# Left-over tokens of a top-1 mixture of experts: first and last item in conditional blocks, the last one in plain float32 column tiles

## The chip, the cores and the metric

One core of one Trainium2 chip runs the whole kernel. The metric is device time in microseconds (us) of one execution, as the median of three runs.

## What is computed

Sigmoid attention over 8 batches of 12 heads with 448 tokens of 64 features, then a mixture of 8 experts over the 3584 tokens of 768 features, where each token goes to its best expert alone. All is float32.

```python
scores = scale * q @ k.T - log(S)
attn = 1 / (1 + exp(-scores));  x = attn @ v        # heads side by side: 3584 x 768
logits = x @ w_gate                                  # 8 experts
expert_idx = argmax(logits);  gate_w = softmax(logits)[expert_idx]
for e in range(8):
    xe = x[expert_idx == e]
    h = maximum(xe @ w1[e], 0)                       # w1[e]: 768 x 1024
    out[expert_idx == e] = gate_w * (h @ w2[e])      # w2[e]: 1024 x 768
```

## The kernel before

Attention runs pair of heads by pair of heads (scores L534, sigmoid L521, weighted values L548), in plain float32 on quadrants of 64 x 64 of TensorE's array. The experts run batch by batch: each batch's 448 tokens go through the expert that most of them chose (w1 at L218, w2 at L237), and the attention of later batches is interleaved with that. Every float32 operand of the experts is cut into a high and a low float32r part (ScalarE casts, L143, VectorE subtracts, L144), and a product is the sum of three matmuls, high x high, high x low, low x high. A unit of weights is such a pair of 512 columns, made from half of a raw tile of 512 KB that SP loads (L136, L166).

Tokens that chose another expert than their batch's are recorded, with gate, in a table in memory (recs). What is left over is done at the end, as items: up to 256 rows of one expert. While the last batch's experts run, VectorE makes the list of items (L706 to L742): items of over 128 rows come first, then the smaller ones; li holds their numbers and experts, ki how many there are of each sort. With the inputs used there are two items, worked out from the reference: 218 rows of expert 7 and 1 row of expert 3.

An item's body is `item(i, nh, ...)` (L843), nh halves of 128 rows. The rows' x is the stationary operand and w1, split into w1h and w1l for all 1024 columns beforehand, moves with 512 columns (L854). Each half of h is turned by four transposes (L900) and split again (L903), since h must be stationary for w2, whose units are split as the body goes on. VectorE or ScalarE multiply by the gate (L938 for VectorE) into xo, and GpSimd writes rows out with two indirect DMAs, the scatter (L810), that are issued at the start of the next item or behind the loops. A table, AT, says behind which matmul of an item each split of weights and of rows stands. So the first item's body also gathers, sorts and turns the rows of the second (L764 to L787), and loads and splits its w1 (L804).

Two hardware loops follow one another: items with nh = 2 (L945), then items with nh = 1 (L947). Every engine reads the loops' bounds from ki (L841) and walks through both loops; a loop's turn is a join of all engines. In the last batch, `until(n)` puts a step n matmuls ahead of that batch's last one, and `more(n)` lets n matmuls go by. There stand the gather of the first item's rows, their sorting and turning, and the loads and splits of its w1. Raw tiles come from a ring of five (wst), behind the last batch also from four tiles (hl) that the batch's h occupied.

Of the kernel before, what the change touches and what calls it, by code (L numbers as in the profile page):

```python
# [25 lines left out]
def tile_sigmoid_attention_top1_moe(  # L26
# [644 lines left out]
    for s, n in attention():  # L671
        if s >= START:
# [8 lines left out]
    ps_m2 = ctx.enter_context(tc.tile_pool(name="ps_m2", bufs=3, space=bass.MemoryType.PSUM))  # L681
    TL = 2 * P


    AT = (
        (
            dict(zip((0, 1, 2, 3, 4, 12, 5, 6, 7, 8, 13, 14, 15, 16, 9, 10, 11, 17),
                     (38, 43, 48, 54, 60, 84, 102, 108, 114, 120, 126, 132, 138, 144, 150, 156, 162, 175))),
            (74, 90, 128, 168),
        ),  # L690
        (dict(zip((0, 1, 4, 5, 8, 9, 2, 3, 6, 7, 10, 11), (16, 20, 24, 28, 33, 42, 48, 54, 60, 66, 72, 78))), ()),
    )
# [18 lines left out]
    big, few, rank = cut(4), cut(5), [cut(6), cut(7)]  # L711
    nc.vector.tensor_tensor(ek(5), ek(0), n_rec, op=ALU.is_lt)
    nc.vector.tensor_scalar(cut(0), cut(0), float(P), None, op0=ALU.add)
    nc.vector.tensor_tensor(ek(4), ek(0), n_rec, op=ALU.is_lt)
    nc.vector.tensor_sub(few, few, big)
    more(20)
    for msk, cum in zip((big, few), rank):
        nc.vector.tensor_tensor_scan(cum, cut(3), msk, 0.0, op0=ALU.mult, op1=ALU.add)
# [4 lines left out]
    for msk, cum in zip((big, few), rank):  # L723
        nc.vector.scalar_tensor_tensor(msk, cum, slot1, msk, op0=ALU.is_equal, op1=ALU.mult)
    more(20)
    nc.vector.tensor_add(big, big, few)
    prod = cut(8, 2).rearrange("p (a n) -> p a n", a=2)
    nc.vector.tensor_mul(
        prod, cut(1, 2).rearrange("p (a n) -> p a n", a=2), big.unsqueeze(1).broadcast_to([P, 2, NI])
# [4 lines left out]
    ki = rest.tile([1, 2], I32, name="ki")  # L734
    nc.vector.tensor_scalar(ends[:, 0:1], ends[:, 1:2], -1.0, ends[:, 0:1], op0=ALU.add, op1=ALU.max)
    nc.vector.tensor_copy(ki, ends[0:1])
# [9 lines left out]
    rec_s = rest.tile([P, 2, 2], U32, name="rec_s")  # L746
    rec_c = rest.tile([P, 2, 2], U32, name="rec_c")
    rec_n = rest.tile([P, 2, 2], U32, name="rec_n")
    xg = rest.tile([P, 2, DM], F32, name="xg")
# [4 lines left out]
    w1h = rest.tile([P, KD, DF], F32R, name="w1h_item")  # L754
    w1l = rest.tile([P, KD, DF], F32R, name="w1l_item")
# [7 lines left out]
    def get_rows(ireg, rec, nh):  # L763
        nc.sync.dma_start(rec, recs_v[bass.ds(ireg, 1)].rearrange("o p t w -> (o p) t w"))  # L764
        for t in range(nh):
# [9 lines left out]
    def sort_rows(nh):  # L775
        for t in range(nh):
            nc.vector.tensor_copy(
                xp[:, t].rearrange("p k (i s) -> p k i s", s=32), xg[:, t].rearrange("p (i k s) -> p k i s", i=4, s=32)
            )

    def split_rows(k2, nh):
        px = ps_x.tile([P, 512], F32, tag="px", name=f"px_{k2}")
        w = nh * P
        for kk in range(2):
            for t in range(nh):
                at = kk * w + t * P
                nc.tensor.transpose(px[:, at : at + P], xp[:, t, 2 * k2 + kk], ident)  # L787
        for kk in range(2):
            xh, xl = xrs[2 * k2 + kk]
            part = px[:, kk * w : (kk + 1) * w]  # L790
            nc.scalar.copy(xh[:, :w], part)
            nc.vector.tensor_sub(xl[:, :w], part, xh[:, :w].bitcast(F32))

    RAWS = [(wpool, "wst")] * RAWS_AHEAD
    turn = itertools.count()

    def raw_tile(name):
        pool, ring = RAWS[next(turn) % len(RAWS)]
        bufs = RAWS_AHEAD if ring == "wst" else None
        return pool.tile([P, 1024], F32, tag=ring, bufs=bufs, name=name)  # L800

    def w1_load(ereg, t):
        st = raw_tile(f"w1r_{t}")
        nc.sync.dma_start(st, w1[bass.ds(ereg, 1), t * P : (t + 1) * P, :].rearrange("e p n -> (e p) n"))  # L804
        return st

    def scatter():
        puts = []
        for t in range(2):
            put = nc.gpsimd.indirect_dma_start(  # L810
                out=out,
                out_offset=bass.IndirectOffsetOnAxis(ap=rec_s[:, t, 0:1], axis=0),
# [7 lines left out]
    nc.gpsimd.iota(rec_s, pattern=[[0, 4]], base=int(BIG), channel_multiplier=0)  # L820
    nc.gpsimd.memset(xg, 0.0)
    get_rows(item_reg(0), rec_c, 2)
    e0 = expert_reg(0)
    until(96)
    sort_rows(2)
    until(86)
    for k2 in range(KD // 2):
        split_rows(k2, 2)
        more(8)
    until(60)  # L830
    w1rs = [w1_load(e0, t) for t in range(3)]
    for t in range(KD):
        until(50 - 9 * t)
        part_split(w1rs[t], (w1h[:, t], w1l[:, t]), nc.vector)
        if t + 3 < KD:
            w1rs.append(w1_load(e0, t + 3))
    until(0)
    next(mo, None)
    order.close()
    RAWS = RAWS + [(hpool, f"hl{j}") for j in range(0, KF, 2)]  # L840
    ends_r = [nc.values_load(ki[0:1, a : a + 1], min_val=0, max_val=NI) for a in range(2)]  # L841

    def item(i, nh, split_at, sort_at):  # L843


        n = 0
        hooks = {}

        def at(m, f):
            hooks.setdefault(m, []).append(f)  # L850

        def mm(*a, **kw):
            nonlocal n
            nc.tensor.matmul(*a, **kw)  # L854
            n += 1
            for f in hooks.pop(n, ()):
                f()

        ereg = expert_reg(i)
        scatter()  # L860
        if sort_at:
            enext = expert_reg(i + 1)
            get_rows(item_reg(i + 1), rec_n, nh)
        raws, parts = {}, {}
        todo = list(dict.fromkeys(u // 2 if u < NU else NU + u for u in split_at))

        def load():
            if todo:
                r = todo.pop(0)
                if r < NU:  # L870
                    raws[r] = raw_tile(f"w2r_{r}")
                    w2_rows(ereg, r, raws[r])
                else:
                    raws[r] = w1_load(enext, r - 2 * NU)

        def split(u):
            if u < NU:
                parts[u] = part_tiles("w2", 512, f"r_{u}")
                part_split(raws[u // 2][:, u % 2 * 512 : (u % 2 + 1) * 512], parts[u], nc.vector)
            else:  # L880
                t = u - NU
                part_split(raws[NU + u], (w1h[:, t], w1l[:, t]), nc.gpsimd if t % 2 else nc.vector)
            if u >= NU or u % 2:
                load()

        for _ in RAWS:
            load()
        for u, m in split_at.items():
            at(m, lambda u=u: split(u))
        half = DF // 2  # L890
        if sort_at:
            at(sort_at[0], lambda: sort_rows(nh))
            for k2 in range(KD // 2):
                at(sort_at[1 + k2], lambda k2=k2: split_rows(k2, nh))
        hts = {}

        def turn_h(f, h, hf):
            ph = ps_x.tile([P, 512], F32, tag="px", name=f"ph_{f}_{h}")
            for c in range(4):
                nc.tensor.transpose(ph[:, c * P : (c + 1) * P], hf[:, c * P : (c + 1) * P], ident)  # L900
            two = hpool.tile([P, 1024], F32R, tag=f"hh{4 * f + 2 * h}", name=f"h_{f}_{h}")
            hh, hl = two[:, :512], two[:, 512:]
            nc.scalar.copy(hh, ph)  # L903
            nc.vector.tensor_sub(hl, ph, hh.bitcast(F32))
            hts[f, h] = hh, hl

        for f in range(2):
            for h in range(nh):
                ps = ps_moe.tile([P, 512], F32, tag="moe", name=f"ps1_{f}_{h}")
                cs = slice(f * half, (f + 1) * half)  # L910
                for t in range(KD):
                    xh, xl = (x[:, h * P : (h + 1) * P] for x in xrs[t])
                    for m, (a, b_) in enumerate(((xh, w1h), (xh, w1l), (xl, w1h))):
                        mm(ps, a, b_[:, t, cs], start=(t == 0 and m == 0), stop=(t == KD - 1 and m == 2))
                hf = opool.tile([P, 512], F32, tag="ob", name=f"hf_{f}_{h}")
                nc.scalar.activation(hf, ps, AF.Relu)
                at(n + 9, lambda f=f, h=h, hf=hf: turn_h(f, h, hf))


        order = [(d, h, jh) for d in range(ND) for h in range(nh) for jh in range(2)]  # L920
        if nh == 1:
            order.sort(key=lambda x: x[2])
        pos = {}
        for d, h, jh in order:
            if jh == 0:
                pos[d, h] = ps_m2.tile([P, 512], F32, tag="m2", name=f"ps2_{d}_{h}")
            ps = pos[d, h][:, :DW]
            for j in range(4):
                whi, wlo = (x[:, j % 2 * DW : (j % 2 + 1) * DW] for x in parts[4 * d + 2 * jh + j // 2])
# [48 lines left out]
```

## Time and profile before

| | us |
|---|---|
| median of 3 runs (smallest to largest) | 850.48 (848.18 to 853.02) |
| the profiled execution's own time | 845.28 |
| its span in the profile | 842.0 |
| last batch's last matmul ends, first item begins | 773.4 |
| first item begins to second item begins | 773.4 to 815.3 |
| second item | 815.3 to 834.0 |
| from there to the end | 834.0 to 842.0 |

The profile shows one execution on the core. PE is TensorE's matmuls, PEld its weight loads, DVE is VectorE, ACT ScalarE, POOL GpSimd, SP the engine that issues most loads. A group of instructions is named by source line, engine, operation, output <- inputs and shape; after the bar stand its busy time and the mean duration of one in ns, then the idle time in front of it and what ended that. The chain that ended last is written in order of time: start, duration, engine, what, line.

### The profile page before, as it was taken

How to read it: one execution, taken by the hardware profiler on the slowest of the kernel's cores; microseconds unless marked ns; L12 is line 12 of the kernel's file. 1: busy time of each engine (PE TensorE's matmuls, PEld its weight loads, DVE VectorE, ACT ScalarE, POOL GpSimd, SP SyncE). 2: the span in 40 equal slices, each digit the busy share in tenths (PEclk: the TensorE clock that was granted, in tenths of full speed). 3: DMA queues.
4: the chain of work that ended last, by engine and by line, in shares of the span. 5: the costliest groups of instructions: out<-in, count | busy, mean ns of one | idle time of the engine just before them, and what ended most of it. 6: DMA issues, size and time to landing. Idle time of an engine off the chain costs nothing.

```text
span 842.0 us, 15396 instructions
## 1 busy us (share of the span) xinstructions
PE 827.2 (98%) x5637; PEld 635.2 (75%) x5637; DVE 415.2 (49%) x863; ACT 398.6 (47%) x691; POOL 154.8 (18%) x221
## 2 busy tenths in 40 slices
PE   8999999999999999999999999999999999999986
PEld 6647678677678677687687687787687689998875
DVE  2456446435464355345464365353472257556544
ACT  5875634454534635445525626435526522334543
POOL 3445003110041002210041001300141005202240
PEclk9999999999999999999999999999999999999998
DMA  8999865485394574784656565675642427537523
GB/s 152 153 185 187 213 146 135 110 206 131 73 220 111 115 168 117 141 185 102 140 123 159 146 127 128 152 157 130 140 135 67 118 58 191 170 119 211 203 81 124
DMA packets 289514, 120.61 MB, mean 143 GB/s; under 512 B 204420, under 2 KB 283156, under 8 KB 289440
## 3 DMA queue, kind: packets, MB, share of 16 engines
q1 hardware_dynamic: 278176, 99.27, 50.9%
q0 software_dynamic: 9088, 19.46, 9.5%
q10 hardware_dynamic: 2176, 0.92, 0.8%
q8 instruction: 44, 0.72, 0.4%
q14 instruction: 30, 0.25, 0.1%
HBM read 97.55 MB, written 24.64 MB: 145 GB/s over the span
## 4 chain that ended last, share of the span: by engine, by line
PE 94%; DMA 3%; issue 1%; DVE 1%; ACT 1%; POOLq 0%; ACTq 0%; POOL 0%; SPq 0%; DVEq 0%
PE ps L237 28%; PE ps L218 28%; PE sc L534 15%; PE av L548 15%; PE ps L854 5%; PE psg L265 2%; DMA kn<-in_k_dram 1%; DMA first<-in_q_dram 1%; DMA out_dram<-ob 1%; DMA w2r<-in_moe_w_dram 0%; PE pl L274 0%; PE ph L900 0%; PE px L787 0%; DVE xt L411 0%; POOLq L973 0%
## 5 line engine op out<-in xcount | busy, mean ns | idle before, releaser
L521 ACT ACTIVATE at<-sc,bias_s 128x448 f32<-128x448 f32 x336 | 196.0, 631 | 133.2 <-PE sc L534 132.0
L534 PE MATMUL sc<-qt,kt 64*64 64x448 f32 x1344 | 174.8, 545 | 0.1
L548 PE MATMUL av<-at,vn 64*64 64x448 f32 x1344 | 173.1, 537 | 0.0
L253 POOL DMA_DIRECT2D out_dram<-ob x96 | 61.1, 649 | 486.2 <-DVE ob L248 407.7
L237 PE MATMUL ps<-hh,w2l 128*128 128x448 f32 x384 | 141.9, 370 | 0.0
L237 PE MATMUL ps<-hh,w2h 128*128 128x448 f32 x384 | 141.6, 369 | 0.0
L218 PE MATMUL ps<-xl,w1h 128*128 128x448 f32 x384 | 141.3, 368 | 0.0
L218 PE MATMUL ps<-xh,w1l 128*128 128x448 f32 x384 | 140.7, 366 | 0.2 <-DVE w1l L144 0.2
L237 PE MATMUL ps<-hl,w2h 128*128 128x448 f32 x384 | 140.8, 367 | 0.0
L218 PE MATMUL ps<-xh,w1h 128*128 128x448 f32 x384 | 140.4, 366 | 0.0
L557 DVE TENSOR_TENSOR xl<-av,xh 128x448 fp32r<-128x448 f32 x48 | 29.0, 605 | 216.4 <-ACT xh L556 215.0
L534 PEld LDWEIGHTS sc<-qt,kt 64*64 64x64 f32 x1344 | 79.7, 191 | 58.2 <-issue 24.0
L223 ACT ACTIVATE hh<-ps 128x448 fp32r<-128x448 f32 x64 | 34.9, 545 | 161.2 <-PE ps L218 161.1
L548 PEld LDWEIGHTS av<-at,vn 64*64 64x64 f32 x1344 | 64.3, 132 | 59.5 <-issue 26.3
L143 ACT CAST w2h<-wst 128x512 fp32r<-128x512 f32 x96 | 61.5, 658 | 86.9 <-PE ps L237 78.7
L218 PEld LDWEIGHTS ps<-xl,w1h 128*128 128x128 f32 x384 | 72.1, 188 | 10.8 <-issue 5.2
L237 PEld LDWEIGHTS ps<-hh,w2h 128*128 128x128 f32 x384 | 72.2, 188 | 9.4 <-issue 4.2
L237 PEld LDWEIGHTS ps<-hh,w2l 128*128 128x128 f32 x384 | 72.2, 188 | 8.3 <-issue 2.8
L218 PEld LDWEIGHTS ps<-xh,w1l 128*128 128x128 f32 x384 | 72.1, 188 | 8.3 <-issue 1.4
L218 PEld LDWEIGHTS ps<-xh,w1h 128*128 128x128 f32 x384 | 72.1, 188 | 6.4 <-issue 0.7
L237 PEld LDWEIGHTS ps<-hl,w2h 128*128 128x128 f32 x384 | 72.2, 188 | 5.6
L144 DVE TENSOR_TENSOR w2l<-wst,w2h 128x512 fp32r<-128x512 f32 x96 | 64.0, 683 | 22.6 <-ACT w2h L143 21.9
(152 smaller groups left out, 809.5 us busy)
## 6 DMA issues: line engine op xcount, KB each, us to landing
wst<-in_moe_w_dram SPq DMA_DIRECT2D x48, 512.0 KB
wst<-in_moe_w_dram SPq DMA_DIRECT2D x56, 384.0 KB
x_tok<-xt SPq DMA_DIRECT2D x64, 168.0 KB
out_dram<-ob POOLq DMA_DIRECT2D x96, 112.0 KB
kn<-in_k_dram SPq DMA_DIRECT2D x184, 56.0 KB
qn<-in_q_dram SPq DMA_DIRECT2D x168, 56.0 KB
vn<-in_v_dram SPq DMA_DIRECT2D x68, 112.0 KB
w1r<-in_moe_w_dram SPq DMA_DIRECT2D x12, 512.0 KB
```

Source lines behind the costliest of these rows:

```text
L143: nc.scalar.copy(hi, st)
L144: eng.tensor_tensor(lo, st, hi.bitcast(F32), op=ALU.subtract)
L218: nc.tensor.matmul(ps[:, :S], a[:, ws], b_, start=(t == 0 and n == 0), stop=(t == KD - 1 and n == 2))
L223: nc.scalar.activation(hh[:, :S], ps[:, :S], AF.Relu)
L237: nc.tensor.matmul(ps[:, :S], a, b_, start=(j == 0 and n == 0), stop=(j == KF - 1 and n == 2))
L253: nc.gpsimd.dma_start(out[b * S : (b + 1) * S, cols].rearrange("(j r) f -> r j f", r=32), obv[32 * i : 32 * (i + 1)])
L265: nc.tensor.matmul(psg[: 2 * E, :S], wgs[:, t], xch[b, t][n], start=(t == 0 and n == 0), stop=(t == KD - 1 and n == 1),)
L521: nc.scalar.activation(at, ps[:, :S], AF.Sigmoid, bias=bias_s, scale=SCALE)
L534: nc.tensor.matmul(ps[quarter(g, h), :S], ks, ops[g, "q"][OWN[h]], start=True, stop=True)
L548: nc.tensor.matmul(psv[g][OWN[h], :S], ops[g, "v"][rows, c, :], at[rows], start=(c == 0), stop=(c == KC - 1))
L557: nc.vector.tensor_sub(xl, pv[:, :S], xh.bitcast(F32))
L854: nc.tensor.matmul(*a, **kw)
```

## The change

The list now sorts items by whether they have over 32 rows (FEW). ki holds five numbers: how many items there are, the index of the last, how many are few (up to 32 rows; only a last item can be treated so, and few ones come last), the number of items if none is few and else 0, and the end of a loop over items between first and last. All engines leave the last batch into straight code with conditional blocks:

- `If(n_items >= 2)`: the first item, as a full one of 256 rows. Its body is now class Item: w1 stationary in blocks of 128 x 128, x moving with 256 columns (L861), which yields h already turned, so that the transposes of h go. Then h is stationary and w2 moves with 256 columns (L881). The 12 raw tiles give 24 units; each serves 12 matmuls, and each is split five units ahead. Nine raw tiles exist (five of the ring, four hl), the last three loads reuse the first three tiles. The scatter stands at the body's end.
- `If(n_few >= 1)`: the last item, if few. Its raw weights wait in 12 kept tiles, loaded for the greater part during the last batch, unsplit. The 32 rows are stationary in column tiles of 32: in each group, matmuls of 256 columns go to 4 (w1, L903) or 3 (w2, L917) column tiles of the array. Between them stand relu, two transposes (L910) and a copy, behind them one multiplication by the gate and one scatter of 96 rows of 256.
- `If(n_full >= 1)`: the last item, if not few, as a full one. Then the loop over the items between, which has no turn with two items.

Into the last batch go, besides: the records of the last item (L936, L938), a second gather (L963), the sorting and six transposes of the few rows (L992), nine loads of kept tiles, nine of raw tiles and the first five splits. 

```diff
-    AT = (...)
+    FEW = 32
...
+    kf = rest.tile([P, 5], F32, name="kf")
+    total = ends[:, 1:2]
+    nc.vector.tensor_copy(kf[:, 0:1], total)
+    nc.vector.tensor_scalar(kf[:, 1:2], total, -1.0, 0.0, op0=ALU.add, op1=ALU.max)
+    nc.vector.tensor_sub(kf[:, 2:3], total, ends[:, 0:1])
...
-    w1h = rest.tile([P, KD, DF], F32R, name="w1h_item")
-    w1l = rest.tile([P, KD, DF], F32R, name="w1l_item")
+    NR = 12
+    kept = [rest.tile([P, 1024], F32, name=f"kept_{r}") for r in range(NR)]
...
+    class Item:
...
+        def split(self, n):
+            while self.done < min(n, self.UNITS):
+                u = self.done
...
+                raw = self.raws[u // 2 % self.slots]
+                part_split(raw[:, u % 2 * 512 : (u % 2 + 1) * 512], self.part(u), nc.vector)
+                self.done += 1
+                again = u // 2 + self.slots
+                if u % 2 and again < NR:
+                    load_raw(raw, e0, again)
...
+                for t in range(KD):
+                    whi, wlo = self.part(u)
+                    xh, xl = xrs[t]
+                    for j in range(4):
+                        js = slice(j * P, (j + 1) * P)
+                        for m, (a, b_) in enumerate(((whi, xh), (whi, xl), (wlo, xh))):
+                            nc.tensor.matmul(
+                                pss[j], a[:, js], b_, start=(t == 0 and m == 0), stop=(t == KD - 1 and m == 2)
+                            )
...
+                    u += 1
+                    self.split(u + self.AHEAD)
...
+            scatter(rec)
+
+    def few_rows():
...
+        for t in range(KD):
+            for g in range(4):
+                raw = raw_view(kept[3 * (g // 2) + t // 2], 512)[:, t % 2, g % 2 * NF : (g % 2 + 1) * NF]
+                nc.tensor.matmul(
+                    ps[FEW * g : FEW * (g + 1), :NF], x_few[:, t], raw, start=(t == 0), stop=(t == KD - 1)
+                )
+        hf, ht, y = (few_t[:, n * NF : (n + 1) * NF] for n in range(3))
+        nc.scalar.activation(hf, ps[:, :NF], AF.Relu)
...
+        for j in range(KF):
+            at = j % 2 * P + j // 2 * FEW
+            for d in range(ND):
+                raw = raw_view(kept[6 + 2 * d + j // 4], DW)[:, j % 4]
+                nc.tensor.matmul(
+                    ps[FEW * d : FEW * (d + 1), :DW], ht[:, at : at + FEW], raw, start=(j == 0), stop=(j == KF - 1)
+                )
+        rows = slice(0, ND * FEW)
+        nc.vector.tensor_scalar(y[rows], ps[rows, :DW], rec_f[:, 1:2].bitcast(F32), None, op0=ALU.mult)
+        nc.gpsimd.indirect_dma_start(
...
+    until(107)
+    load_some(None, 0, 1, None, 2, None, 3, 4)
...
     until(60)
-    w1rs = [w1_load(e0, t) for t in range(3)]
+    load_some(None, 5, None, 6, 7, 8)
...
+    for t in range(KD):
+        nc.tensor.transpose(px[:, t * FEW : (t + 1) * FEW], xs[:, t], ident[:FEW, :FEW])
...
+    load_some(None, None, None, None)
...
-    with tc.For_i(0, ends_r[0]) as i, tc.manual_schedule():
-        item(i, 2, *AT[0])
-    with tc.For_i(ends_r[0], ends_r[1]) as i, tc.manual_schedule():
-        item(i, 1, *AT[1])
-    scatter()
+    with tc.If(n_items >= 2), tc.manual_schedule():
+        one.run(rec_c)
+    for r in range(9, NR):
+        last_raw(r)
+    with tc.If(n_few >= 1), tc.manual_schedule():
+        few_rows()
+    with tc.If(n_full >= 1), tc.manual_schedule():
...
+    with tc.For_i(1, n_end) as i, tc.manual_schedule():
...
```

(In `load_some`, None is a raw tile of the first item, a number a kept tile of the last.)

SP's queue in the last batch, from the registers for the first item's number and expert (li) to the next load of that batch's own w2, tile 10 of its ring (wst_10). Before:

```order
L758 TENSOR_LOAD li
L758 ISA x2
L764 ISA
L764 DMA rec_c<-recs 128x2x2
L761 TENSOR_LOAD li
L761 ISA x2
L136 ISA
L136 DMA wst_10_8031<-in_moe_w_dram 128x4x256
```

The same place on SP now:

```order
L775 DMA rec_c<-recs 128x2x2
L763 TENSOR_LOAD li
L763 ISA x2
L934 TENSOR_LOAD ki
...
L760 TENSOR_LOAD li
...
L763 TENSOR_LOAD li
...
L936 DMA rec_n<-recs 128x2x2
...
L938 DMA rec_f<-recs 32x2
...
L136 DMA wst_10_8079<-in_moe_w_dram 128x4x256
```

Between the load of rec_c and that of wst_10 now stand three more register loads (the last item's index, number and expert) and four more DMAs: rec_n, and rec_f three times.

PE's queue where the first item's turn of the loop ends and the second item begins. ki is what the register load reads, ps_warm an idle matmul. Before:

```order
L512 MATMUL ps_warm<-ones 128x128
L945 REGISTER_ALU
L945 COMPARE_AND_BRANCH
L945 UNCONDITIONAL_BRANCH
L841 TENSOR_LOAD ki
L947 COMPARE_AND_BRANCH
L947 UNCONDITIONAL_BRANCH x2
L973 BRANCH_PREFETCH_HINT
L854 MATMUL ps_0_0_8954<-w1h_item,rxh_7982 128x512
```

The same place on PE now, from the first item's last matmul to the first of the few rows:

```order
L881 MATMUL ps_2_1_8900<-w2h_r_8491,hr_8523 128x256
L1006 UNCONDITIONAL_BRANCH x2
L1003 TENSOR_LOAD ki
L1010 COMPARE_AND_BRANCH
L903 MATMUL few_8964<-kept_8002,x_few 32x256 x2
L903 MATMUL few_8964<-kept_8005,x_few 32x256 x2
```

The end of the loop has gone from between the two, a register load and a branch are left, and the matmuls behind them are of another kind: 32 output rows, raw weights of a kept tile as the moving operand.

More of the change, by code (lines that the diff above doesn't have):

```diff
@@ L710, in tile_sigmoid_attention_top1_moe @@
     n_rec = base.unsqueeze(2).broadcast_to([P, E, NK])
-    big, few, rank = cut(4), cut(5), [cut(6), cut(7)]
+    full, few, rank = cut(4), cut(5), [cut(6), cut(7)]
     nc.vector.tensor_tensor(ek(5), ek(0), n_rec, op=ALU.is_lt)
-    nc.vector.tensor_scalar(cut(0), cut(0), float(P), None, op0=ALU.add)
+    nc.vector.tensor_scalar(cut(0), cut(0), float(FEW), None, op0=ALU.add)
     nc.vector.tensor_tensor(ek(4), ek(0), n_rec, op=ALU.is_lt)
-    nc.vector.tensor_sub(few, few, big)
+    nc.vector.tensor_sub(few, few, full)
     more(20)
-    for msk, cum in zip((big, few), rank):
+    for msk, cum in zip((full, few), rank):
         nc.vector.tensor_tensor_scan(cum, cut(3), msk, 0.0, op0=ALU.mult, op1=ALU.add)
@@ L789, in split_rows, with scatter @@
             xh, xl = xrs[2 * k2 + kk]
[L790 to L807, printed above, removed]
+            part = px[:, kk * TL : (kk + 1) * TL]
+            nc.scalar.copy(xh, part)
+            nc.vector.tensor_sub(xl, part, xh.bitcast(F32))
+    def scatter(rec):
         puts = []
@@ new lines, in few_rows @@
+    def few_rows():
+        ps = ps_m2.tile([P, 512], F32, tag="m2", name="few_1")
+        NF = DF // 4
+        for t in range(KD):
[3 more added lines that the diff above has]
+                    ps[FEW * g : FEW * (g + 1), :NF], x_few[:, t], raw, start=(t == 0), stop=(t == KD - 1)
+                )
+        hf, ht, y = (few_t[:, n * NF : (n + 1) * NF] for n in range(3))
+        nc.scalar.activation(hf, ps[:, :NF], AF.Relu)
+        px = ps_x.tile([P, 512], F32, tag="px", name="few_px")
+        for c in range(2):
+            nc.tensor.transpose(px[:, c * P : (c + 1) * P], hf[:, c * P : (c + 1) * P], ident)
+        nc.scalar.copy(ht, px[:, :NF])
+        ps = ps_m2.tile([P, 512], F32, tag="m2", name="few_2")
+        for j in range(KF):
+            at = j % 2 * P + j // 2 * FEW
+            for d in range(ND):
+                raw = raw_view(kept[6 + 2 * d + j // 4], DW)[:, j % 4]
+                nc.tensor.matmul(
+                    ps[FEW * d : FEW * (d + 1), :DW], ht[:, at : at + FEW], raw, start=(j == 0), stop=(j == KF - 1)
+                )
+        rows = slice(0, ND * FEW)
+        nc.vector.tensor_scalar(y[rows], ps[rows, :DW], rec_f[:, 1:2].bitcast(F32), None, op0=ALU.mult)
+        nc.gpsimd.indirect_dma_start(
+            out=out.rearrange("n (d f) -> (n d) f", d=ND),
+            out_offset=bass.IndirectOffsetOnAxis(ap=at_f[:, 0:1], axis=0),
+            in_=y[rows],
+            in_offset=None,
+            bounds_check=ND * NT - 1,
+            oob_is_err=False,
+        )
@@ L821, in tile_sigmoid_attention_top1_moe @@
     nc.gpsimd.memset(xg, 0.0)
-    get_rows(item_reg(0), rec_c, 2)
+    get_rows(item_reg(0), rec_c)
     e0 = expert_reg(0)
-    until(96)
-    sort_rows(2)
+    last = nc.sync.value_load(ki[0:1, 1:2], min_val=0, max_val=NI - 1)
+    i_last, e_last = item_reg(last), expert_reg(last)
+    nc.sync.dma_start(rec_n, recs_v[bass.ds(i_last, 1)].rearrange("o p t w -> (o p) t w"))
+    for d in range(ND):
+        nc.sync.dma_start(
+            rec_f[FEW * d : FEW * (d + 1)], recs_f[bass.ds(i_last, 1), 0].rearrange("o p w -> (o p) w")
+        )
@@ new lines, in tile_sigmoid_attention_top1_moe, with first_raw, last_raw, load_some @@
+    SLOTS = [(wpool, "wst")] * RAWS_AHEAD + [(hpool, f"hl{j}") for j in range(0, KF, 2)]
+    raws = []
+    def first_raw():
+        r = len(raws)
+        pool, ring = SLOTS[r]
+        bufs = RAWS_AHEAD if ring == "wst" else None
+        raws.append(pool.tile([P, 1024], F32, tag=ring, bufs=bufs, name=f"raw_{r}"))
+        load_raw(raws[r], e0, r)
+    def last_raw(r):
+        load_raw(kept[r], e_last, r)
+    def load_some(*todo):
+        for r in todo:
+            first_raw() if r is None else last_raw(r)
@@ L826, in tile_sigmoid_attention_top1_moe @@
+    until(107)
+    load_some(None, 0, 1, None, 2, None, 3, 4)
+    until(96)
+    sort_rows()
+    for t in range(2):
+        nc.gpsimd.indirect_dma_start(
+            out=xg[:, t, :],
+            out_offset=None,
+            in_=x_tok,
+            in_offset=bass.IndirectOffsetOnAxis(ap=rec_n[:, t, 0:1], axis=0),
+            bounds_check=NT - 1,
+            oob_is_err=False,
+        )
     until(86)
     for k2 in range(KD // 2):
-        split_rows(k2, 2)
+        split_rows(k2)
         more(8)
@@ L830, in tile_sigmoid_attention_top1_moe @@
     until(60)
-    w1rs = [w1_load(e0, t) for t in range(3)]
+    load_some(None, 5, None, 6, 7, 8)
+    until(46)
+    one = Item(raws, len(SLOTS))
+    one.split(1)
+    until(34)
+    one.split(2)
+    xs = wpool.tile([P, DM], F32, tag="w1h", bufs=RING["w1"], name="few_x")[:FEW].rearrange("p (k f) -> p k f", f=P)
+    sorted_row(xs, xg[:FEW, 0])
+    few_t = wpool.tile([P, DM], F32, tag="w1l", bufs=RING["w1"], name="few_t")
+    nc.vector.tensor_copy(row_f[:, 0:1], rec_f[:, 0:1])
+    nc.vector.scalar_tensor_tensor(row_f[:, 1:2], block[: ND * FEW, 2:3], 2.0, block[: ND * FEW, 1:2], op0=ALU.mult, op1=ALU.add)
@@ L832, in tile_sigmoid_attention_top1_moe @@
+    nc.vector.scalar_tensor_tensor(at_f, row_f[:, 0:1], float(ND), row_f[:, 1:2], op0=ALU.mult, op1=ALU.add)
+    until(22)
+    one.split(3)
+    px = ps_x.tile([P, 512], F32, tag="px", name="px_few")
     for t in range(KD):
[L833 to L836, printed above, removed]
+        nc.tensor.transpose(px[:, t * FEW : (t + 1) * FEW], xs[:, t], ident[:FEW, :FEW])
+    nc.scalar.copy(x_few.rearrange("p t r -> p (t r)"), px[:, : KD * FEW])
@@ L837, in tile_sigmoid_attention_top1_moe @@
+    until(10)
+    one.split(4)
     until(0)
     next(mo, None)
+    load_some(None, None, None, None)
+    h_two.extend(hpool.tile([P, 1024], F32R, tag=f"hh{n}", name=f"hr_{n}") for n in range(0, KF, 2))
+    one.split(5)
     order.close()
[L840 to L857, printed above, removed]
-        ereg = expert_reg(i)
-        scatter()
[L861 to L929, printed above, removed]
-                hh, hl = (x[:, j * P : (j + 1) * P] for x in hts[jh, h])
-                for m, (a, b_) in enumerate(((hh, whi), (hh, wlo), (hl, whi))):
-                    mm(ps, a, b_, start=(jh == 0 and j == 0 and m == 0), stop=(jh == 1 and j == 3 and m == 2))
-            if jh == 1:
-                to, gate = xo[:, h, d * DW : (d + 1) * DW], rec_c[:, h, 1:2].bitcast(F32)
-                if d == 1:
-                    nc.scalar.mul(to, ps, gate)
-                else:
-                    nc.vector.tensor_scalar(to, ps, gate, None, op0=ALU.mult)
-        if sort_at:
-            warm_up(10)
-        nc.vector.tensor_copy(rec_s, rec_c)
-        if sort_at:
-            nc.vector.tensor_copy(rec_c, rec_n)
@@ new lines, in tile_sigmoid_attention_top1_moe @@
+    with tc.If(n_full >= 1), tc.manual_schedule():
+        sort_rows()
+        for k2 in range(KD // 2):
+            split_rows(k2)
+        it = Item(kept)
+        it.split(it.AHEAD)
+        it.run(rec_n)
+    with tc.For_i(1, n_end) as i, tc.manual_schedule():
+        ereg = expert_reg(i)
+        get_rows(item_reg(i), rec_c)
+        for r in range(NR):
+            load_raw(kept[r], ereg, r)
+        sort_rows()
+        for k2 in range(KD // 2):
+            split_rows(k2)
+        it = Item(kept)
+        it.split(it.AHEAD)
+        it.run(rec_c)
```

107 lines of the change are left out of this document (77 added, 30 removed).

## The prediction, made before the changed kernel had run

> **What bounds the kernel now.** I read the page's busy rows first, then the chain of work that ended last, then windows cut at the borders of the stages.
>
> ```profile
> span 842.0 us, 15396 instructions
> PE 827.2 (98%) x5637; PEld 635.2 (75%) x5637; DVE 415.2 (49%) x863; ACT 398.6 (47%) x691; POOL 154.8 (18%) x221
> ```
>
> TensorE (PE) works 98% of the span, so time is won only where PE does less or stands still less. The change touches the part behind the last batch. The windows give, from left, length, busy time (and instructions) of PE, its weight loads, VectorE, ScalarE and GpSimd, then granted clock, DMA share and GB/s:
>
> ```profile
> 741.30:773.40 32.10, 32.10 (x165) 29.71 (x164) 21.33 (x30) 13.10 (x20) 5.12 (x8) 1.00 0.46 136
> 773.40:815.30 41.90, 38.37 (x256) 34.23 (x255) 22.58 (x35) 19.37 (x34) 14.64 (x11) 1.00 0.45 157
> 815.30:834.00 18.70, 18.34 (x116) 16.24 (x116) 10.06 (x16) 9.64 (x17) 2.02 (x2) 1.00 0.60 205
> 834.00:842.00 8.00, 0.00 (x0) 0.00 (x0) 0.24 (x2) 0.00 (x0) 1.94 (x2) 0.72 0.02 3
> ```
>
> The first item takes 41.9 us, the second 18.7, the end 8.0: together 68.6 us, of which PE stands still 3.5 in the first item and all 8 at the end. The chain over the same stretch shows where:
>
> ```profile
> 795.08 4.55 PE ps L854 x38
> ...
> 800.07 3.36 PE ps L854 x28
> ...
> 805.83 1.33 issue
> 807.16 0.69 DVE w2l_r L144
> ...
> 813.11 0.48 DVE xo L938
> ...
> 813.95 1.31 issue
> 815.27 6.56 PE ps L854 x27
> ...
> 826.09 7.57 PE ps L854 x63
> 833.68 0.06 DVE xo L938
> ...
> 835.34 0.97 POOL out_dram L810
> 836.31 1.28 POOLq L973
> ```
>
> PE waits 2 us for a late split (805.83), 1.31 us at the turn from one loop to the next (813.95), and the end hangs on two scatters.
>
> **The change part by part.** *First item.* It now issues 2 halves x 6 x 4 x 3 = 144 matmuls of w1 and 3 x 4 x 2 x 2 x 3 = 144 of w2, all 256 columns wide. The row at 800.07 has 28 such in 3.36 us, 0.12 each: 288 x 0.12 = 34.6 us. No transposes, no warm-ups and no loads of the next item stand between them. What feeds them is one split of 512 columns per 12 matmuls, 1.44 us:
>
> ```profile
> L144 DVE TENSOR_TENSOR w2l_r<-w2r,w2h_r 128x512 fp32r<-128x512 f32 x24 | 15.8, 687 | 11.6 <-ACT w2h_r L143 11.4
> L143 ACT CAST w2h_r<-w2r 128x512 fp32r<-128x512 f32 x24 | 14.2, 620 | 9.9 <-DMA w2r<-in_moe_w_dram 9.4
> ```
>
> 0.69 on VectorE and 0.62 on ScalarE fit into 1.44, with five pairs ahead; if a pair came late, PE would lose up to 1.3 us for each. I allow 0.4 for the turn between the halves. The loads are as many as before, 24 of 512 KB, and stand earlier on SP:
>
> ```profile
> 741.32 23.24 SPq L804 DMA_DIRECT2D w1r<-in_moe_w_dram  x6
> 815.30:827.00 11.70, 11.70 (x62) 9.80 (x63) 5.00 (x8) 5.86 (x11) 2.02 (x2) 1.00 0.88 300
> ```
>
> At the 300 GB/s of the second row a load takes 1.75 us. Raw tiles 5 to 8 lie in memory that the last batch reads until 773.4; with the one in front of them they land by 773.4 + 5 x 1.75 = 782.2. Tile 5 feeds units 10 and 11, used from 788.2. The cover is 6 us, and the three last kept tiles land by 790 for use at 813.
>
> *Ahead of 773.4.* On PE six transposes of the few rows come in:
>
> ```profile
> 821.83 0.44 PE ph L900 x4
> ```
>
> Four of 128 columns cost 0.44, so I take 0.4 for six narrow ones, at most 0.66. SP gets three register loads and four small DMAs ahead of the last batch's load of w2 tile 10 (the first of the pieces shown with the change):
>
> ```profile
> 724.30 0.37 SPq L764 DMA_DIRECT2D rec_c<-recs  x1
> 727.17 11.47 SPq L136 DMA_DIRECT2D wst<-in_moe_w_dram  x4
> 739.92 1.21 ACT L143 CAST w2h<-wst 128x512 fp32r<-128x512 f32 x2
> L841 SPq TENSOR_LOAD <-ki x2: 266/268/270, 720.7 to 721.3; - x2
> ```
>
> Four issues of 0.37 and three register loads of some 0.5 with their arithmetic move that load from 727.2 to about 730.2; its first split is the second cast at 739.92, at 740.5, and a load takes 2 to 4 us. Nothing on PE moves; without this cover each us would count.
>
> *From the first item to the last.* Before, PE leaves the loop only when all engines have:
>
> ```profile
> L945 PEldq EVENT_SEMAPHORE  x12: 51/51/560, 812.2 to 814.0; - x12
> L841 PEldq TENSOR_LOAD <-ki x2: 316/404/493, 770.8 to 814.4; - x2
> 773.44 0.39 PE L854 MATMUL ps<-w1h_item,rxh 128*128 128x512 f32 x1
> ```
>
> In the changed program a register load and a branch are all that stands on PE between the items (the second piece shown with the change). The join with other engines is gone there. At 770.8 such a load ran 2.6 us ahead of its matmul (773.44) and cost nothing; the loop turn cost 1.31. Ends 0 and 1.31; I take 0.5, nearer the first row, which is the same pair of instructions.
>
> *Last item.* The second item goes: 18.7 us. In come 24 + 24 plain float32 matmuls of 256 columns in column tiles of 32, which before has nowhere. The nearest rows are attention's plain float32 quadrants of 64 x 64, 448 columns:
>
> ```profile
> 60.30 0.93 PE L548 MATMUL av<-at,vn 64*64 64x448 f32 x8
> 61.05 0.93 PE L534 MATMUL sc<-qt,kt 64*64 64x448 f32 x8
> L548 PEld LDWEIGHTS av<-at,vn 64*64 64x64 f32 x1344 | 64.3, 132 | 59.5 <-issue 26.3
> ```
>
> Eight records, four matmuls of the program (1344 records for 672), start every 0.75 us: four run side by side, and two that share rows of the array have different moving data. Scaled to 256 columns a group takes 0.43, by four passes of 0.12 each 0.48; I take 0.45. First product: 6 groups, 2.7 us. Second: 8 groups of three, 3.6. If tiles don't run side by side, 48 x 0.45 = 21.6 in place of 6.3. Between the products stand relu, two transposes and a copy:
>
> ```profile
> 784.00 0.60 ACT L916 ACTIVATE hf<-ps 128x512 f32<-128x512 f32 x1 [3.05 <-DMA out_dram<-ob]
> 784.65 0.66 PE L900 MATMUL ph<-ident,hf 128*128 128x128 f32 x4
> 785.53 0.59 ACT L903 CAST h<-ph 128x512 fp32r<-128x512 f32 x1
> ```
>
> That is 2.1 us at 512 columns; at 256, 1.6. None of it is covered.
>
> A rule speaks against this part: the Trainium skill (TensorE: Matmul & The Clock Gate, The mechanism) says that weight loads overlap matmuls in flight only where the row groups differ, and column tiles share all rows. The trace disagrees: eight loads of 132 ns or more and eight matmuls fit into 0.75 us. By the rule 48 x 2 x 0.132 = 12.7 us would be added, and the forecast would be 844.8.
>
> *End.* The gate on VectorE costs 0.48, as at 813.11. GpSimd starts 0.3 behind it, as here:
>
> ```profile
> 754.63 1.09 DVE L248 TENSOR_TENSOR ob<-ob,gt 128x896 f32<-128x896 f32 x1
> 756.02 2.61 POOL L253 DMA_DIRECT2D out_dram<-ob  x4 [25.92 <-DVE ob L248]
> ```
>
> Before, 6.7 us pass from the first scatter (835.34) to 842.0, the second 1.28 behind; one scatter leaves 5.4. The exit of the loop of no turns now stands behind the landing: four semaphore rows of 51 ns, 0.2. Ends: 4.1, if the second scatter cost twice 1.28, and 6.9, if it cost nothing.
>
> *Sum.* 773.4 + 0.4 + 34.6 + 0.4 + 0.5 + 2.7 + 1.6 + 3.6 + 0.5 + 0.3 + 5.6 = 823.6, against 842.0: 18.4 us less. The profiled execution took 845.28, 3.28 outside its span; it would take 826.9. The median of the runs shown is 850.48 (848.18 to 853.02), 5.2 above it; 850.48 - 18.4 = 832.1, and I say 832.
>
> **The rivals.**
> - *Column tiles two at a time.* For: four moving streams share each row, and attention shows two. Against: nothing in a row. Groups cost 0.9; 6 x 0.9 and 8 x 0.9 in place of 6.3 add 6.3: 838.
> - *Column tiles one after another,* or their weight loads not hidden. 21.6 in place of 6.3, +15.3: 847; by 132 ns a load, 845. Against: the quadrants.
> - *Far branches.* After its last matmul PE jumps over two skipped item bodies. Before has only near branches, so a far one has no row. The nearest is the way of a weight load from issue to first use:
>
> ```profile
> 815.47 5.68 SPq L136 DMA_DIRECT2D w2r<-in_moe_w_dram  x6
> 819.54 0.62 ACT L143 CAST w2h_r<-w2r 128x512 fp32r<-128x512 f32 x1 [8.44 <-DMA w2r<-in_moe_w_dram]
> ```
>
> At 4.1 us each PE would be through at 817.2 + 8.2 + 0.5 = 825.9, when GpSimd, ready at 822.8, would have waited 3.1: 835. It decides from about 2.5 us each. The Trainium skill (Runtime: NRT & Kernel Launch, Instruction fetch mechanics) says that a taken branch out of the window of two pages waits for its code to be fetched; no run here shows it yet.
> - *The loads become the bound: slower.* 12.6 MB from 741.3 must be there by 813. If the 136 GB/s of the first window were the limit and not the demand, and contention made it 130, the last kept tile would land at 838.1, and 1.8 + 0.5 + 0.3 + 5.6 behind it end at 846.3: 854.8. It decides at about 136. Against: 300 GB/s in the row at 815.30.
> - *The last item isn't few: slower.* Over 32 rows it would take a full item: 808.8 + 0.5 + 4 for turning its rows + 34.6 + 8.0 = 855.9, so 864. Against: in the end's window the DMA queue of the scatters
>
> ```profile
> q0 software_dynamic: 160, 0.00, 1.0%
> ```
>
> moves 0.00 MB for two tiles of up to 128 rows of 3 KB; 33 rows would be 0.10.
>
> **How the numbers follow.** Forecast 0.60 (its own range 828 to 836: the ends of the change of items, of the end and of 0.43 to 0.48 are worth 2 us down and 2 up, the spread of the runs shown as much); two at a time 0.13; one at a time 0.10; far branches 0.10; loads 0.04; a full item 0.03. From 827 to 841 lie the forecast, far branches and two at a time, 0.83. About 0.5%, 4.3 us, is what a measurement of this kernel can tell from no change. Faster by more (under 846.2): 0.60 + 0.13 + 0.10 and half of one at a time, 0.88; within: the rest of it, 0.05; slower: 0.07.
>
> **What would show it.** Right: 288 matmuls at 0.12 from about 773.8 to 808.8 with no wait for splits; first matmul of the last item within 1 us; 6 groups in 2.7 us and 8 in 3.6; under 6 us from the scatter to the end. Wrong: groups of 0.9 or 1.8 us, waits of PE for kept or raw tiles, queue gaps behind the last matmul, or a start of the first item later than 774.5.

## The result, and the profile after

The changed kernel takes 830.86 us (median of 4 runs, 830.0 to 831.49), the kernel before beside it 850.64: a ratio of 0.977, 95% interval 0.974 to 0.980. The forecast was 832 (827 to 841). The profiled execution took 831.49 with a span of 829.8; the sum had 826.9 and 823.6. So the time came out as forecast and the span did not, and it takes the pieces to see why.

The page of the changed kernel, and its windows by stage: the two products of the first item, the few rows up to the issue of their scatter, the end.

```profile
span 829.8 us, 15348 instructions
```

```profile
777.31:794.60 17.29, 17.29 (x146) 17.29 (x146) 11.30 (x19) 9.36 (x19) 2.51 (x4) 1.00 0.89 302
794.60:811.80 17.20, 17.20 (x145) 17.06 (x144) 7.45 (x14) 6.60 (x13) 0.00 (x0) 1.00 0.01 1
811.80:820.55 8.75, 6.89 (x99) 3.52 (x98) 0.96 (x2) 0.76 (x2) 2.08 (x3) 1.00 0.21 79
820.55:829.80 9.25, 0.00 (x0) 0.00 (x0) 0.00 (x0) 0.00 (x0) 0.94 (x1) 0.56 0.03 7
```

The first item is as forecast: TensorE is busy in every us of it, 34.5 us in place of 41.9. The few rows in the timeline:

```profile
811.80 2.80 PE L903 MATMUL few<-kept,x_few 128*32 128x256 f32 x48
...
814.69 0.38 ACT L907 ACTIVATE few_t<-few 128x256 f32<-128x256 f32 x1 [3.03 <-PE few L903]
...
816.03 3.65 PE L917 MATMUL few<-kept,few_t 128*32 128x256 f32 x48 [0.46 <-ACT few_t L911]
819.79 0.48 DVE L921 TENSOR_SCALAR few_t<-few,rec_f 96x256 f32<-96x256 f32 x1 [7.40 <-PE few L917]
820.55 0.94 POOL L922 DMA_INDIRECT out_dram<-few_t,at_f  x1 [6.22 <-DVE few_t L921]
```

Six groups in 2.80 us and eight in 3.65 (forecast 2.7 and 3.6). Then the scatter starts at 820.55, and the end takes 9.25 us where 5.6 stood in the sum. The queues of TensorE and GpSimd behind it, by line (duration min/median/max in ns, first and last start in us; L1012 is the block of the full last item, L1019 the loop of no turns, L1053 the program's end):

```profile
L1012 PEldq COMPARE_BRANCH  x1: 3767/3767/3767, 818.5 to 818.5; - x1
L1012 POOLq INC_SWDGE_SEM  x1: 1000/1000/1000, 821.1 to 821.1; - x1
```

```profile
L1019 POOLq EVENT_SEMAPHORE  x14: 17/43/43, 822.6 to 824.9; - x14
...
L1019 PEldq COMPARE_BRANCH  x3: 78/197/3999, 823.0 to 828.7; - x3
L1019 POOLq INC_SWDGE_SEM  x1: 954/954/954, 822.7 to 822.7; - x1
```

```profile
L1053 POOLq DRAIN  x3: 46/109/3332, 825.1 to 829.5; - x3
...
L1053 PEldq DRAIN  x2: 8/8/8, 828.9 to 829.3; - x2
```

Two things stand here behind the last scatter that before had not there: TensorE jumps twice over skipped code, 3.77 and 4.00 us, and GpSimd takes a counter step of 1.0 us at each skipped body and walks through 14 semaphore rows, so that its drain of 3.33 us starts only at 825.1. The drain ends at 828.4; TensorE, behind its second jump and a walk of its own, reaches its first closing row at 828.9. So TensorE comes last, by 0.5 us, but the two ways are nearly equally long, and this profile alone doesn't say what either is worth.

### The profile page after: what moved, and what is told of

Same layout as the page of the kernel before. It is cut to its first block, busy times and chain, and to the rows that moved or that the text cites. A ratio compares the mean times of both kernels' runs of the same rounds, so it can differ in the third digit from the quotient of the medians.

```text
span 829.8 us, 15348 instructions
## 1 busy us (share of the span) xinstructions
PE 814.9 (98%) x5659; PEld 623.4 (75%) x5659; DVE 398.9 (48%) x851; ACT 383.7 (46%) x672; POOL 144.3 (17%) x214
## 4 chain that ended last, share of the span: by engine, by line
PE 94%; DMA 2%; SPq 2%; issue 1%; POOL 0%; POOLq 0%; DVE 0%; DVEq 0%
PE ps L237 29%; PE ps L218 29%; PE sc L534 15%; PE av L548 14%; PE psg L265 2%; PE ps L881 2%; PE ps L861 2%; SPq L457 1%; DMA kn<-in_k_dram 1%; DMA qn<-in_q_dram 1%; DMA first<-in_k_dram 1%; DMA out_dram<-xo,rec_c 0%; PE pl L274 0%; SPq L497 0%; SPq L471 0%
```

## Theories and experiments

Theory A: GpSimd's steps through the skipped block and the loop hold back its drain, and the jumps lie beside them. Theory B, the rival of the prediction: TensorE's jumps set the end. In the table stand the medians, and of the profiled runs (one of each kernel) the time from the start of the last scatter to the start of GpSimd's long drain, and to the end of the span. Theories are told apart by the last two columns, since the medians of these kernels, from separate groups of 4 or 5 runs, also scatter by where the first item starts.

| kernel | median us | scatter to drain | scatter to end |
|---|---|---|---|
| changed | 830.86 | 4.55 | 9.25 |
| short_bodies | 829.64 | 3.4 | 7.6 |
| no_full | 829.32 | 3.4 | 7.6 |
| no_loop | 828.28 | 1.5 | 5.7 |
| one_if | 827.10 | 1.7 | 5.8 |
| two_blocks | 826.35 | 1.3 | 5.5 |
| no_bodies | 825.38 | 0 | 5.1 |

**no_bodies**

```diff
-    with tc.If(n_full >= 1), tc.manual_schedule(): ...
-    with tc.For_i(1, n_end) as i, tc.manual_schedule(): ...
```

> The full last item and the loop of the items between, both skipped with these inputs, are left out of the program. Theory (TensorE's two jumps of 3.8 and 4.0 us over them set the end): from the issue of the last scatter to the end 5.4 us in place of 9.25, so 3.8 us less than the changed kernel, a median of 827. Rival (the end hangs on GpSimd's drain and the scatter's landing, and the jumps lie beside them): 830.4 to 831.4, no change.

Measured 825.38 (ratio to before 0.972, 0.968 to 0.976). The end falls to 5.1 us; something in the two bodies costs 4.2. This doesn't yet tell A from B, since both go.

**short_bodies**

```diff
     with tc.If(n_full >= 1), tc.manual_schedule():
-        sort_rows(); split_rows(...)
-        it.run(rec_n)
+        it.run(rec_n, range(1))      # first half of w1 alone, no scatter
     with tc.For_i(1, n_end) as i, tc.manual_schedule():
-        sort_rows(); split_rows(...)
-        it.run(rec_c)
+        it.run(rec_c, range(2))      # w1 alone, no scatter
```

> The structure of blocks and loop stays, with all its joins, but the skipped bodies are shorter on TensorE: 72 matmuls in the block, 144 in the loop, in place of 288 with the turning of rows (what is left out is never executed with these inputs). Theory A (GpSimd's own steps through the loop of no turns, ahead of its drain, set the end; TensorE's jumps lie beside them): 8.7 to 9.2 us from the last scatter to the end, 830.3 to 831.4. Theory B (the two long jumps set the end): if they fall to under 0.5 us each, the end takes 5.4 to 5.8 and the median is 827 to 827.5; if only the shorter falls, 829. Both expect the jump over 72 matmuls to be shorter than 3.8 us.

TensorE's jumps and GpSimd's drain in this kernel (L1013 the block, L1017 the loop):

```profile
L1013 PEldq COMPARE_BRANCH  x1: 347/347/347, 818.0 to 818.0; - x1
```

```profile
L1017 PEldq COMPARE_BRANCH  x3: 70/188/1455, 820.0 to 823.1; - x3
L1017 POOLq COMPARE_BRANCH  x3: 38/38/39, 821.0 to 823.4; - x3
L1017 POOLq INC_SWDGE_SEM  x1: 1005/1005/1005, 821.1 to 821.1; - x1
```

```profile
L1048 POOLq DRAIN  x3: 46/109/3332, 823.5 to 827.4; - x3
```

The jumps fell from 3.77 and 4.00 to 0.35 and 1.46 us, 6 us together, and TensorE is through at 823.4. The end still takes 7.6: that the jumps count in full falls. Theory A had said 8.7 to 9.2: since the short body has no scatter, the block has no counter step on GpSimd, and 1.15 of the 1.67 us is the drain that starts as much sooner. The other 0.5 is what the second jump did cost: from the drain's start to the end it is 4.1 to 4.2 us here and in the other kernels of the table that have a block or a loop, 4.7 in the changed kernel.

So this edit shortened GpSimd's way as well as TensorE's. A kernel made for another question, column_by_column (below), tells the two apart: it has the same block and loop and jumps as long, 3.57 and 4.04 us, but its first jump begins 3.8 us ahead of the last scatter, not 2.0. Its closing rows, with the scatter at 831.85 and the end at 840.6:

```profile
L1053 POOLq DRAIN  x3: 46/109/3332, 836.4 to 840.3; - x3
...
L1053 PEldq DRAIN  x2: 8/8/8, 838.4 to 840.1; - x2
```

GpSimd's drain starts 4.55 us behind the scatter, just as in the changed kernel; TensorE is through at 838.4, ahead of the drain's end at 839.7; and the end takes 8.7 us. So GpSimd's way alone makes 8.7, and TensorE's adds 0.5 to it in the changed kernel.

**no_full and no_loop**: the block, or the loop, taken out of the program alone.

> The full last item is left out of the program (it is not executed with these inputs), the loop of no turns stays. Theory A (GpSimd's steps through the loop set the end): a skipped block costs GpSimd one counter step of 1.0 us and no more, so 8.2 to 8.7 us from the last scatter to the end, a median of 829.8 to 830.5. Theory B (each long jump counts in full): 5.4 to 5.8 us, 827 to 827.5.

> The loop of the items between is left out (it makes no turn with these inputs), the full last item stays in its skipped block, with its jump of 3.8 us on TensorE. Theory A (GpSimd's steps through the loop set the end): 5.7 to 5.9 us from the last scatter to the end, 3.4 less, a median of 827.3 to 827.6. Theory B (each long jump counts in full): the same here, so that this run and the one without the full item are alike; by theory A they differ by 2.5 to 3 us.

The jump and the drain without the loop:

```profile
L1012 PEldq COMPARE_BRANCH  x1: 3598/3598/3598, 820.0 to 820.0; - x1
L1012 POOLq COMPARE_BRANCH  x1: 50/50/50, 822.3 to 822.3; - x1
L1012 POOLq INC_SWDGE_SEM  x1: 1005/1005/1005, 822.6 to 822.6; - x1
```

```profile
822.06 0.94 POOL L922 DMA_INDIRECT out_dram<-few_t,at_f  x1 [6.15 <-DVE few_t L921]
```

```profile
L1042 POOLq DRAIN  x3: 46/109/3332, 823.6 to 827.5; - x3
```

Without the loop a jump of 3.6 us is left, and the end takes 5.7 all the same: the jump is over at 823.6, when GpSimd's drain begins, and costs nothing. Without the full item the end takes 7.6 (theory A had 8.2 to 8.7: it had taken off the counter step of 1.0, not the 0.5 by which TensorE came last). GpSimd gains no more there because it now has to wait 0.51 us in one row of the loop's walk:

```profile
L1012 POOLq EVENT_SEMAPHORE  x14: 17/43/513, 820.6 to 823.4; - x14
```

Without the loop the end is 3.5 us shorter, without the block 1.65, without both 4.2 (9.25 to 5.1). The 0.5 of the second jump is in each of the three, and the counter step that comes first lies in part beside the scatter's own 0.94 us. The medians (829.32 and 828.28) lie closer together than the ends, because the start scatters (see before_again).

**one_if and two_blocks**: the full last item goes into the loop, and the loop into one conditional block. In the second, both conditions come from one number, the items that are not done as few.

```diff
-    with tc.If(n_full >= 1), tc.manual_schedule(): ...
-    with tc.For_i(1, n_end) as i, tc.manual_schedule(): ...
+    with tc.If(n_big >= 2):
+        with tc.For_i(1, n_big) as i, tc.manual_schedule(): ...
```

> The full last item goes into the loop (it runs to the last item that isn't few), and the loop stands inside one conditional block, so that one jump is left in place of two and no engine joins another at the loop. Theory (each jump costs its full length unless GpSimd's drain lies beside it): the one jump from about 818.5 to 822.3 lies beside the scatter and the drain, the end comes 3.3 to 3.8 us earlier, a median of 827 to 827.6. Rival (the drain or the landing sets the end): 830.4 to 831.4, no change. Second rival (TensorE is not through before the jump and the drain waits for it): 828.5 to 830.

> One conditional block around the loop as in the run with one block, with the conditions for the first item and the loop taken from one number (the count of items that aren't done as few rows), so that it holds for every list of items. By both theories it does what that run did: 827.1, within 0.6.

Measured 827.10 (0.974, 0.970 to 0.978) and 826.35 (0.974, 0.972 to 0.977): a skipped block costs GpSimd one counter step, a loop inside it nothing. two_blocks is written for every list of items (it ran with this one) and beats both kernels: the one before beside it (848.97) by 22.6 us, the changed one by 3.8 us of end (9.25 to 5.5; the medians, from separate groups of runs, differ by 4.5).

**column_by_column**: does the gain of the few rows come from column tiles that run side by side?

```diff
-        for t in range(KD):
-            for g in range(4):
+        for g in range(4):
+            for t in range(KD):
```

and the same exchange of j and d in the second product.

> The same 48 matmuls of the few rows, in another order: all of one column tile behind one another, then the next tile, so that neighbours never lie in different tiles. Theory (tiles run side by side only as neighbours in the queue, and a plain float32 matmul of 256 columns takes 0.43 to 0.47 alone): 24 take 10.3 to 11.2 us in place of 2.80, and 24 more in place of 3.65, so 14 to 16 us more, a median of 845 to 847. Rival (a matmul of 32 output rows is simply cheap, 0.12 to 0.15 each): 830.4 to 831.4, no change.

Its timeline:

```profile
812.75 8.05 PE L903 MATMUL few<-kept,x_few 128*32 128x256 f32 x48
...
822.17 8.88 PE L917 MATMUL few<-kept,few_t 128*32 128x256 f32 x48 [0.46 <-ACT few_t L911]
```

Median 840.21, 9.4 us more. The rival falls: narrow outputs aren't cheap by themselves, neighbours in different tiles make them so. (This order also puts matmuls that add to the same sums behind one another. That this is what slows them was not tried apart; the first item's matmuls, float32r, do so three by three at 0.12 us each.) But a tile alone takes 0.335 and 0.370 us a matmul, not 0.43: the expected size was off. Four abreast take 2.80 / 6 = 0.467 a group, three 3.65 / 8 = 0.456, so four run 2.9 times as fast as one, not four times.

**loop_of_one**: was it the join at the loop's turn that stood between the items?

```diff
-    with tc.If(n_items >= 2), tc.manual_schedule():
+    with tc.For_i(0, n_few) as _, tc.manual_schedule():
         one.run(rec_c)
```

> The first item stands in a loop of one turn, as in the kernel before, in place of its conditional block. Theory (the join of all engines at the loop's end is what stood between the items): the gap on TensorE from the first item's last matmul to the first of the few rows, 0.09 us in the changed kernel, becomes 2.5 to 4, since GpSimd's two scatters now stand ahead of the join; the median 833 to 835. Rival (the gap before was TensorE's own register load and branch): 0.1 to 0.5, no change. A second question: the time outside the span, 1.7 us in the changed kernel and 3.3 before. If a loop that makes a turn is what makes it longer, it is 3.3 here.

The chain, the timeline, and two windows (the few rows' products):

```profile
815.88 2.95 DMA out_dram<-xo,rec_c
```

```profile
820.43 4.45 PE L903 MATMUL few<-kept,x_few 128*32 128x256 f32 x48 [5.99 <-issue]
```

```profile
820.40:825.00 4.60, 4.45 (x48) 2.01 (x48) 0.00 (x0) 0.02 (x1) 0.00 (x0) 0.63 0.88 287
826.30:830.00 3.70, 3.65 (x48) 1.88 (x48) 0.00 (x0) 0.00 (x0) 0.00 (x0) 1.00 0.04 11
```

Median 839.95, 9.1 more. A join there does make TensorE stand, and is dearer than I said: it waits until the first item's scatter has landed (815.88 + 2.95 = 818.83) and then walks on for 1.6 us, so TensorE stands 5.99 us, and then its clock is granted at 0.63, which makes 4.45 of 2.80 us. These two make 7.6 of the 9.1 us. The Trainium skill (TensorE: Matmul & The Clock Gate, Part 1) says that an idle window of some 3.4 us halves the clock and as long a busy one restores it; the rows agree: 0.63 over 4.6 us is what 3.4 us at half speed give, and 1.00 follows. The second question stays open: 2.1 us lie outside the span here.

**first_alone and last_full**: the part of the few rows taken out, and replaced by a full item.

```diff
 first_alone: the block of the few rows, all kept loads, the full block and the loop are removed
 last_full:
-    nc.vector.tensor_scalar(cut(0), cut(0), float(FEW), None, op0=ALU.add)
+    nc.vector.tensor_scalar(cut(0), cut(0), 0.0, None, op0=ALU.add)
```

> The last item is left out, with its twelve kept loads, its block, the full block and the loop (its one row of output is not computed). Theory: the kept loads cost the last batch nothing, so TensorE takes 51.6 to 52.4 us from the list's matmuls to the first item, as in the changed kernel and its variants; behind the first item's last matmul stand the gate, two scatters and 5.1 to 5.8 us of end, so the few rows' part is worth 10 to 11 us in all, a median of 819.5 to 821. Rival (the kept loads slow the last batch): 51.0 to 51.4 us from the list to the first item.

> The list's border is 0 rows in place of 32, so that the last item is done as a full one, from its kept tiles, and the block of the few rows is skipped. The prediction's rival gave 864 for this; with what the tail measured (8.75 us of few rows and 9.25 of end go, 4 for turning the rows, 34.5 for the matmuls and 9.5 to 10.5 for two scatters and the loop come) it is 860 to 862. Slower than the kernel before, either way.

first_alone: 818.60, under the 819.5 to 821 expected, so the part is worth 12.3 us with the end that it brings, not 10 to 11. last_full: 869.95, 8 above the upper end of what was expected and 6 above the prediction's rival. Its windows (turning of the rows, then the first matmuls) show the miss:

```profile
809.90:822.00 12.10, 5.46 (x21) 4.29 (x22) 6.23 (x13) 4.73 (x11) 1.94 (x2) 0.65 0.01 2
822.00:840.00 18.00, 18.00 (x146) 18.00 (x145) 10.63 (x21) 9.77 (x20) 0.00 (x0) 0.95 0.00 1
```

From the first item's end to a running product pass some 10 us, not 4, since nothing hides sorting, turning and the first splits, and TensorE's clock is granted at 0.65 there. The matmuls take some 2 us more than 34.5, the first of them at a lower clock too. Together that is the 8 us.

**before_again**: where does the late start of the changed kernel's first item come from?

> The kernel before, unchanged, for a second profile. Theory (the start scatters from run to run): its first item begins somewhere between 773 and 779 us, later than the 773.4 of the first profile by about what its own time is longer. Rival (the changed program itself reaches its first item 3.9 us later): it begins at 773 to 774 again, whatever its own time. Both expect a median between 848 and 853 us.

Its median is 847.13 (10 runs, 845.52 to 851.73). The list's matmuls by line, in before, before_again, the changed kernel and first_alone:

```profile
L740 PE MATMUL pli<-ident,lf x4: 270/272/272, 722.4 to 722.8; 128*1 128x128 f32 x4
```

```profile
L740 PE MATMUL pli<-ident,lf x4: 271/272/273, 723.5 to 723.8; 128*1 128x128 f32 x4
```

```profile
L738 PE MATMUL pli<-ident,lf x4: 271/272/273, 724.9 to 725.2; 128*1 128x128 f32 x4
```

```profile
L738 PE MATMUL pli<-ident,lf x4: 271/272/273, 723.0 to 723.4; 128*1 128x128 f32 x4
```

The first item's first matmul begins at 773.4, 775.1, 777.2 and 775.3: 51.0, 51.6, 52.3 and 52.3 us later. So the place of the list scatters with the run (722.4 and 723.5 in before, 723.0 to 727.4 in the changed kernel and its variants), and the first profile of before was a quick one. From the list on, the changed kernel and its variants all take 51.7 or 52.3 us: the change adds some 0.7 us. Without kept loads it is no shorter (52.3): they cost the last batch nothing, and that rival falls.

The theory was right only in part. The second profile's own time is 4.2 us longer (849.45 to 845.28), but its first item begins only 1.7 later. The other 2.5 lie behind: from the first item's start to the end it takes 71.1 us, the first profile 68.6, and TensorE's granted clock is 0.96 in the first item, where it was 1.00. So the end of the kernel before, on which the prediction's sum rests, scatters as well.

**loads_late**

```diff
-    until(107)
-    load_some(None, 0, 1, None, 2, None, 3, 4)
     until(60)
+    load_some(None, 0, 1, None, 2, None, 3, 4)
     load_some(None, 5, None, 6, 7, 8)
```

> The first eight loads of raw weights are issued with the second six, 60 matmuls ahead of the end of the last batch instead of 107, some 11 us later. Theory (loads run at 300 GB/s, 1.75 us each, and have some 6 us of cover): raw tile 5 is the fifteenth of them and lands at about 790, used from 791.7, so 0 to 1.5 us more, a median of 830.5 to 832.5. Rival (loads run at 130 GB/s behind the last batch, 4 us each, and are nearly the bound): TensorE waits 10 us or more for them in the first item, over 840.

Inconclusive. Median 832.68 (829.34 to 832.86), TensorE waits for no load, but the edit did not delay the loads: the first goes out here at 745.5, in the changed kernel at 744.07, and the list's matmuls, too, begin 1.4 us later here (726.3 to 724.9).

```profile
L770 SPq DMA_DIRECT2D raw<-in_moe_w_dram x6: 373/373/376, 745.5 to 778.2; - x6
```

SP's loads stand in the same order in both kernels: between the two places no other SP instruction stood, so moving them among the matmuls changed nothing on SP. How much cover the loads have was not tried. That they aren't bound at 130 GB/s is plain from the first window of the changed kernel, 302 GB/s.

## Why the prediction was right, point by point

- *First item*, 34.6 + 0.4 and 0.5 to the next: 34.5 measured, no wait for a split, 0.1 to the next item. Of the two ends for the change of items the lower was true; loop_of_one shows that a join at that place makes TensorE stand. The item began at 777.2, past the 774.5 that the prediction named as a sign of being wrong: by before_again some 0.7 of that is the change (0.4 forecast), the rest is scatter, 2.4 us of it ahead of the list. The load of wst_10 moved by 2.8 us against that of rec_c (3.0 forecast), and TensorE waited for nothing in the last batch.
- *Few rows*, 2.7 + 1.6 + 3.6 + 0.5 + 0.3 = 8.7 to the scatter: 8.75. Column tiles run side by side (0.467 and 0.456 a group, 0.45 forecast), and the rivals of two at a time and one after another fall. The rule of the Trainium skill that the prediction weighed (TensorE: Matmul & The Clock Gate, The mechanism) would have made the 48 matmuls 12.7 us longer, by the prediction's estimate; the trace disagrees here too: 48 weight loads of 0.11 us and the 48 matmul records of the first product fit into 2.80 us.
- *End*, 5.6 (4.1 to 6.9): 9.25, outside both ends. This is the step that failed: "The exit of the loop of no turns now stands behind the landing: four semaphore rows of 51 ns, 0.2." I looked at TensorE's rows alone, and counted four where the row that I show for the loop before has x12. GpSimd has a counter step of 1.0 us and a walk of 14 rows there. On GpSimd the loop holds back the drain by 3.0 us (4.55 to 1.5), the skipped block by 1.15, and TensorE's second jump adds 0.5. The 5.4 without all that was nearly right: no_bodies has 5.1.
- *Far branches*: true in mechanism, wrong in price. The jumps took 3.77 and 4.00 us, well over the 2.5 from which they were to decide, but the first begins 1.2 us ahead of the last matmul's end and lies beside the scatter, the second beside the drain: 0.5 in place of 3.1. The Trainium skill (Runtime: NRT & Kernel Launch, Instruction fetch mechanics) says that a taken branch out of the window waits for a fetch. The rows agree in so far as a jump takes longer over a longer body: 0.35 over 72 matmuls, 1.46 over 144, 3.3 to 4.2 over 288 and their turning, about 0.05 on the engines with short bodies. In the window of the second jump (823.2 to 827.4) nothing but two packets of the DMA queue for instructions move, 0.03 MB; for which engine, the row doesn't say.
- *Why the time still fits.* In good part by luck. Four misses cancel: the end +3.65, the item -1.0, the time outside the span, which I carried over as 3.28 and which is 1.7 now (-1.6), and the base. The sum's 18.4 becomes 18.4 - 3.65 + 1.0 + 1.6 = 17.3; measured are 19.8 against the first runs of before, and 17.7 to 18.1 against the medians of before in the later groups of runs (848.54, 848.76, 848.97). The base could account for that difference: with the 71.1 us of before_again in place of 68.6 the 17.3 would be 19.8.

## What to carry to other kernels

Price what stands behind the last useful instruction on every engine's queue, not on the busiest: a hardware loop that makes no turn still sends every engine through a dozen semaphore rows, and on GpSimd holds back the drain. Where two engines' ways to the end are nearly equally long, shortening one of them alone gains little. A body that is seldom needed belongs in one conditional block, loop included, at the place where the longest closing step lies beside its jump. For few rows, matmuls in column tiles run side by side only if neighbours in the queue go to different tiles (10.5 us here).

## What the runs showed of the hardware

- A skipped block with an indirect DMA costs GpSimd 1.0 us (INC_SWDGE_SEM), a loop of no turns 3.0 ahead of its drain.
- GpSimd's closing drain takes 3.33 us in every kernel of the table but no_bodies. There it begins ahead of the scatter's issue, takes 4.37, and ends 3.34 behind the issue's end.
- A jump over skipped code on TensorE: 0.35 us for 72 matmuls, 1.46 for 144, 3.3 to 4.2 for 288 and turning.
- Plain float32 matmuls of 256 columns in column tiles of 32: 0.335 to 0.370 us alone, 0.456 for three abreast, 0.467 for four.
- Outside the span lie 3.2 to 3.6 us in all runs of the kernel before, 1.6 to 2.0 in the changed one and its variants, 2.1 to 2.2 with a loop that makes a turn. What makes it is open.
